# Last head group reordered, its last two heads scaled at Wo's output, and gate and input put into the late tiles' sums early: an attention and MLP gate kernel on one core

## The chip, the cores and the metric

The kernel runs on one core of a Trainium2 chip. The metric is the device time of one execution in microseconds (us), the median of three runs. The core has a matrix engine (PE, which loads weights in a second row called PEld), a vector engine (DVE), an activation engine (ACT), a general engine (POOL), and a queue engine (SP), which issues most transfers.

## The reference

One normalized input feeds an attention over a key and value cache with 32 heads, and a gate made by a two-layer block with shifted channels. The output is the input plus the product of both.

```python
xn = _layernorm(x, axis=-1)                       # x: 1 x 2048 x 512
s = _A_ref(xn, A_k_cache, A_v_cache, A_wq, A_wo)
g = _silu(_B_ref(xn, B_w1, B_w2, B_w3, B_w4))
return x + s * g

def _A_ref(x, k_cache, v_cache, wq, wo):
    q = (lambda x, *d: x.transpose(*d))((x @ wq).reshape(B, Sq, H, Dh), 0, 2, 1, 3)
    scores = jnp.einsum("bhqd,bhkd->bhqk", q, k_cache) * (Dh ** -0.5)
    p = _softmax(scores, axis=-1)
    o = jnp.einsum("bhqk,bhkd->bhqd", p, v_cache)
    return (lambda x, *d: x.transpose(*d))(o, 0, 2, 1, 3).reshape(B, Sq, H * Dh) @ wo
```

There are 2048 queries, 2048 keys, 32 heads of 128 channels, and 512 model channels. The softmax is computed without subtracting a maximum.

## The kernel before, in words

The first stage (before the attention loop) makes the layer norms, the gate for each of 16 tiles of 128 tokens, which stays in `xall`, and the first queries.

The attention is a list of 128 *units*. A unit is one head (`hh`, four in a group) for one block of 512 queries (`qt`, four blocks). The groups `g` run from 0 to 7, and within a group the order is block by block, head by head (`units`, L116). Each unit has eight *slots* (`SPU`), and the main loop (L533) walks slot by slot. The loop's body is the order of instructions on every engine: `pin` keeps instructions in program order, so what stands first in the body goes first on its engine.

In a slot of unit `u`:

- `s_slot` (L272): two score matmuls (called S) of 512 columns into a PSUM tile, and one exponential on ACT into a quarter of the probabilities (`pT`). Two such PSUM tiles rotate.
- `pv_slot` (L302): two value matmuls (called PV), five slots (`LAG`) behind, into `o` of the unit.
- slots 0 and 1: two each of the four matmuls for the next unit's query, and in slot 2 its copy out of PSUM on the DVE (`q_copy`, L264).
- `add_first`, `add_next`, `add_last` (L286 to L300): the DVE sums the probability tiles of the unit down to 128 x 512 in `acc`. The last of them runs in slot 0 of the next unit.
- slot 3: `sums` (L312) of the previous unit. Four matmuls with one column of ones give the sums over keys, the DVE takes reciprocals, and a transfer writes these to memory (`dr`).
- slot 4: `bcast` (L323) reads them back, spread over all 128 partitions (`rb`).
- slot 2: `norm` (L328) of the unit before the previous one. It multiplies `o` with `rb` into `oT`.
- slots 4, 5 and 6: one token tile of Wo's product for a finished block of four heads, by `wo_mm` (L343, four matmuls) and `wo_post` (L358), which adds it into `sacc`. The tiles wait in `wo_todo`.

In the last group `wo_post` also finishes its tile on the DVE: it multiplies by half of the gate (L369), adds the input (L371), which `fin_load` brought by POOL's transfer queue, and SP stores the tile (L372). After the last score slot the loop runs on for three units' length with what is left, and the remaining Wo tiles follow one by one.

PSUM has eight banks: four for the scores, two for `o` (`psO`), one named `xa` that the queries and the sums share, and one named `xm` for Wo.

Of the kernel before, what the change touches and what calls it, by code (L numbers as in the profile page):

```python
# [8 lines left out]
ACT = mybir.ActivationFunctionType  # L9
ALU = mybir.AluOpType  # L10
FP32 = mybir.dt.float32
BF16 = mybir.dt.bfloat16
# [5 lines left out]
def kernel(  # L18
# [26 lines left out]
    QT = Sq // 512  # L45
# [5 lines left out]
    HG = 4  # L51
    NG = H // HG

    SPU = KC // 2
    LAG = 5
# [6 lines left out]
    pin = tc.keep_in_program_order  # L62

    def pool(name, bufs=1, space=None, **kw):
        if space is not None:
            kw["space"] = space
        return tc.tile_pool(name=name, bufs=bufs, **kw)

    ent = ctx.enter_context
    const = ent(pool("const"))  # L70
    xnT = const.tile([P, DC, Sq], BF16, name="xnT")
    xall = const.tile([P, NT, D], BF16, name="xall")
    ones_t = const.tile([P, 1], BF16, name="ones_t")
    nhalf = const.tile([P, 1], FP32, name="nhalf")
    mv1 = const.tile([P, NT, nc.vector.BN_AGGR_DIM], FP32, name="mv1")
    mv2 = const.tile([P, NT, nc.vector.BN_AGGR_DIM], FP32, name="mv2")
# [22 lines left out]
    xsrc = x2d.rearrange("(t p) d -> t p d", p=P)  # L99
# [5 lines left out]
    def mm(out, lhsT, rhs, start, stop):  # L105
        pin(nc.tensor.matmul(out=out, lhsT=lhsT, rhs=rhs, start=start, stop=stop))  # L106

    pin(nc.vector.memset(warm[:], 0.0))
    pin(nc.vector.memset(ones_t[:], 1.0))
    pin(nc.vector.memset(nhalf[:], -0.5))  # L110
    pin(nc.gpsimd.iota(diag[:], pattern=[[-1, P]], base=0, channel_multiplier=1,
                       allow_small_or_imprecise_dtypes=True))
    pin(nc.vector.tensor_scalar(
        out=ident[:], in0=diag[:], scalar1=0.0, scalar2=None, op0=ALU.is_equal))

    units = [(g, qt, hh) for g in range(NG) for qt in range(QT) for hh in range(HG)]  # L116
    NU = len(units)
    NS = NU * SPU
    kTs, vBs, wqs, wos, oTs, st = {}, {}, {}, {}, {}, {}
    todo = defaultdict(list)  # L120

    def at(n, fn):
        todo[n].append(fn)
# [161 lines left out]

    def add_first(u):  # L286
        s = st[u]
        s["acc"] = pB.tile([P, 4, 512], BF16, tag="acc", bufs=2, name="acc")
        pin(nc.vector.tensor_tensor(  # L289
            out=s["acc"][:], in0=s["pT"][0][:], in1=s["pT"][1][:], op=ALU.add))  # L290

    def add_next(u, i):
        a = st[u]["acc"]
        pin(nc.vector.tensor_tensor(out=a[:], in0=a[:], in1=st[u]["pT"][i][:], op=ALU.add))  # L294
# [7 lines left out]
    def pv_slot(u, p):  # L302
        g, qt, hh = units[u]
        s = st[u]
        if p == 0:
            s["o"] = psO.tile([P, 512], FP32, tag="ps_o", name="ps_o")
        pT = s["pT"][p // 2]
        for j in range(2):
            kc = 2 * p + j
            mm(s["o"][:], vBs[g * HG + hh][:, kc, :], pT[:, 2 * (p % 2) + j, :], kc == 0, kc == KC - 1)  # L310
# [10 lines left out]
        pin(nc.sync.dma_start(out=s["dr"][:], in_=rc[:]))  # L321

    def bcast(u):  # L323
        st[u]["rb"] = pB.tile([P, 512], FP32, tag="rb", bufs=2, name="rb")
        pin(nc.sync.dma_start(
            out=st[u]["rb"][:], in_=st[u]["dr"][:].rearrange("p j -> (p j)").partition_broadcast(P)))

    def norm(u):  # L328
        g, qt, hh = units[u]
        s = st.pop(u)  # L330
        if hh == 0:
            oTs[(g, qt)] = pB.tile([P, HG, 512], BF16, tag="oT", bufs=2, name="oT")
        pin(nc.vector.tensor_tensor(  # L333
            out=oTs[(g, qt)][:, hh, :], in0=s["o"][:], in1=s["rb"][:], op=ALU.mult))

    wo_box = {}
    sacc = {}
# [2 lines left out]
        wos[h] = pB.tile([P, D], BF16, tag="wo", bufs=2 * HG, name="wo_h")  # L340
        pin(nc.sync.dma_start(out=wos[h][:], in_=A_wo[h * Dh:(h + 1) * Dh, :]))

    def wo_mm(g, t, hhs, ps=None):  # L343
        if hhs[0] == 0:
            wo_box[0] = psX.tile([P, D], FP32, tag="xm", name="ps_wo") if ps is None else ps
        oT = oTs[(g, t // 4)]
        ts = t % 4
        for hh in hhs:
            mm(wo_box[0][:], oT[:, hh, ts * P:(ts + 1) * P], wos[g * HG + hh][:], hh == 0, hh == HG - 1)

    fin = {}

    def fin_load(t):
        xl = tokp.tile([P, D], BF16, tag="ta", bufs=10, name="xl")
        pin(nc.gpsimd.dma_start(out=xl[:], in_=xsrc[t]))  # L355
        fin[t] = xl

    def wo_post(g, t):  # L358
        ps = wo_box.pop(0)
        if g == 0:  # L360
            sacc[t] = pS.tile([P, D], FP32, tag="sacc", bufs=NT, name="sacc")
            pin(nc.vector.tensor_copy(out=sacc[t][:], in_=ps[:]))
            return
        sa = sacc[t][:]
        pin(nc.vector.tensor_tensor(out=sa, in0=ps[:], in1=sa, op=ALU.add))  # L365
        if g < NG - 1:
            return
        xl, gl = fin.pop(t), xall[:, t, :]
        pin(nc.vector.scalar_tensor_tensor(  # L369
            out=gl, in0=sa, scalar=0.5, in1=gl, op0=ALU.mult, op1=ALU.mult))  # L370
        pin(nc.vector.tensor_tensor(out=xl[:], in0=gl, in1=xl[:], op=ALU.add))  # L371
        pin(nc.sync.dma_start(out=out2d[t * P:(t + 1) * P, :], in_=xl[:]))  # L372

# [121 lines left out]
    pB = left.enter_context(pool("pB", reuse_waits="tile"))  # L495
# [6 lines left out]
    for g in range(NG - 1):  # L502
        b = (g * QT + QT - 1) * HG
        for hh in range(HG):
            h = (g + 1) * HG + hh
# [24 lines left out]
            at(n + 4, lambda: gate_silu(t, th["a"]))  # L530

    wo_todo = deque()
    for n in range(NS + 3 * SPU):  # L533
        u, p = divmod(n, SPU)
        if u < NU:
            g, qt, hh = units[u]
            s_slot(u, p)
        m = n - LAG
        if 0 <= m < NS:
            pv_slot(*divmod(m, SPU))  # L540
        if p in (0, 1) and 4 * HG - 1 <= u < NU - 1:
            q_mm(u + 1, (2 * p, 2 * p + 1))
        if p == 0 and 1 <= u <= NU:
            add_last(u - 1)
        if p == 2 and 4 * HG - 1 <= u < NU - 1:
            q_copy(u + 1)
        if p == 2 and 2 <= u <= NU + 1:
            norm(u - 2)
            if units[u - 2][2] == HG - 1:
                gg, qq = units[u - 2][:2]  # L550
                wo_todo.extend((gg, 4 * qq + ts) for ts in range(4))
                if gg == NG - 1:
                    fin_load(4 * qq)
        if p == 3 and 1 <= u <= NU:
            sums(u - 1)
        if p == 4 and 1 <= u <= NU:
            bcast(u - 1)
        if p in (4, 5) and wo_todo:
            wo_mm(*wo_todo[0], (0, 1) if p == 4 else (2, 3))
        if p == 6 and wo_todo:  # L560
            gg, t = wo_todo.popleft()
            wo_post(gg, t)
            if gg == NG - 1 and t % 4 < 3:
                fin_load(t + 1)
        if p == 4 and u < NU:
            add_first(u)
        if p == 6 and u < NU:
            add_next(u, 2)
        held_mm(n)
        for fn in todo.pop(n, ()):  # L570
            fn()
        if not held and not todo.get(n + 1) and pS is None and n >= 4 * SPU + 5:
            right.close()
            pS = right.enter_context(pool("pS", side="right", reuse_waits="tile"))
    while wo_todo:
        gg, t = wo_todo.popleft()
        wo_mm(gg, t, (0, 1, 2, 3))
        if t not in fin:
            fin_load(t)
        wo_post(gg, t)  # L580
    left.close()
    right.close()

# [29 lines left out]
```

## Time and profile before

| What | us |
|---|---|
| median of three runs | 1286.09 (1286.05 to 1286.43) |
| the profiled execution, its own time | 1285.54 |
| its span in the profile | 1283.8 |
| exponentials on ACT, mean of one (L283, 1024 of them) | 1.027 |
| adds of the probabilities on DVE, mean of one (L294) | 1.221 |
| last add steps on DVE (L299, L300) | 0.692, 0.426 |
| norm on DVE (L333) | 0.681 |
| query copy on DVE (L267) | 0.684 |
| Wo's add on DVE (L365) | 0.692 |
| transfer of reciprocals, out and back, medians | 1.4, 4.1 |
| output store, median from issue to landing | 1.8 |

The span runs from the first instruction to the last event of one profiled execution. The time of that execution lies 1.74 us over its span. A matmul's own duration in the trace includes the filling of the array, so a matmul of 512 columns shows 0.379 us, though the next can start 0.216 us behind it. Groups of instructions are named by line, engine, and output from input. In the chain of waits, each row is the work that the next row waited for.

### The profile page before, as it was taken

Reading aid. Unit: us, or ns where it says so; the run is one execution under the profiler, and the core shown is the slowest. Engines: PE = TensorE matmul, PEld = TensorE weight load, DVE = VectorE, ACT = ScalarE, POOL = GpSimd, SP = SyncE. Lnnn points to the kernel's source line nnn. Section 1 sums busy time; section 2 is a strip of 40 time slices with the busy share of each in tenths; the row PEclk is TensorE's granted clock in tenths of the full one; section 3 lists DMA queues with packets and bytes.
Section 4 is the critical chain, followed back from the end, with each engine's and each line's share of the span. In section 5 each row is a group of like instructions: output and inputs, shape, how many; then the busy total and the mean of one; then the engine's idle time right before and its main releaser. Section 6 shows DMA issues by size and latency. Waiting matters only on the chain.

```text
span 1283.8 us, 16912 instructions
## 1 busy us (share of the span) xinstructions
PE 1263.9 (98%) x6268; PEld 611.3 (48%) x6268; DVE 942.8 (73%) x1316; ACT 1056.8 (82%) x1105; POOL 43.1 (3%) x107
## 2 busy tenths in 40 slices
PE   8999999999999999999999999999999999999996
PEld 4444444444444444444444444444444444444442
DVE  7621567777777777777777777777777777778886
ACT  5444789998888888888888888888888888888882
POOL 4310000000000000000000000000000000000000
PEclk9999999999999999999999999999999999999996
DMA  9391112453144413452144313451244213442221
GB/s 205 56 176 48 24 43 50 82 100 66 33 83 83 83 33 63 79 99 50 42 83 87 70 43 70 79 100 34 50 91 83 58 50 77 80 83 45 63 43 48
DMA packets 169363, 91.05 MB, mean 71 GB/s; under 512 B 122752, under 2 KB 151936, under 8 KB 169280
## 3 DMA queue, kind: packets, MB, share of 16 engines
q1 hardware_dynamic: 165440, 85.24, 33.1%
q0 software_dynamic: 1440, 3.93, 1.4%
q8 instruction: 49, 0.80, 0.3%
q10 hardware_dynamic: 2400, 0.79, 0.2%
q14 instruction: 34, 0.28, 0.1%
HBM read 67.63 MB, written 2.36 MB: 55 GB/s over the span
## 4 chain that ended last, share of the span: by engine, by line
PE 92%; DVE 5%; ACT 1%; DMA 1%; issue 0%; POOL 0%; DVEq 0%; ACTq 0%
PE ps_s L106 37%; PE ps_o L106 35%; PE ps_wo L106 9%; PE ps_q L106 8%; DVE acc L294 2%; PE ps_m L106 2%; PE ps_sum L106 1%; DVE sacc L365 1%; DVE xall L369 1%; DVE acc L299 1%; DVE qT L267 0%; DVE xl L371 0%; DMA rb<-dr 0%; ACT pT L283 0%; ACT xnT L191 0%
## 5 line engine op out<-in xcount | busy, mean ns | idle before, releaser
L283 ACT ACTIVATE pT<-ps_s 128x1024 bf16<-128x1024 f32 x1024 | 993.2, 1027 | 135.2 <-PE ps_s L106 135.2
L106 PE MATMUL ps_s<-qT,kT 128*128 128x512 bf16 x2048 | 609.7, 379 | 1.3 <-ACT pT L283 1.2
L106 PE MATMUL ps_o<-pT,vb 128*128 128x512 bf16 x2048 | 608.4, 379 | 0.0
L294 DVE TENSOR_TENSOR acc<-acc,pT 128x2048 bf16<-128x2048 bf16 x256 | 312.5, 1221 | 72.3 <-ACT pT L283 71.1
L106 PEld LDWEIGHTS <-kT 128*128 128x128 bf16 x2048 | 222.7, 114 | 201.9 <-issue 6.1
L106 PEld LDWEIGHTS <-vb 128*128 128x128 bf16 x2048 | 200.2, 98 | 225.8
L289 DVE TENSOR_TENSOR acc<-pT 128x2048 bf16<-128x2048 bf16 x128 | 156.8, 1225 | 51.1 <-ACT pT L283 51.1
L106 PE MATMUL ps_wo<-wo_h,oT 128*128 128x512 bf16 x512 | 155.6, 388 | 5.4 <-DVE sacc L365 3.1
L106 PE MATMUL ps_q<-xnT,wq_h 128*128 128x512 bf16 x512 | 148.3, 379 | 0.0
L365 DVE TENSOR_TENSOR sacc<-ps_wo,sacc 128x512 f32<-128x512 f32 x112 | 77.5, 692 | 90.0 <-PE ps_wo L106 90.0
L299 DVE TENSOR_TENSOR acc<-acc 128x1024 bf16<-128x1024 bf16 x128 | 88.6, 692 | 4.4
L333 DVE TENSOR_TENSOR oT<-ps_o,rb 128x512 bf16<-128x512 f32 x128 | 87.2, 681 | 1.9 <-DMA rb<-dr 1.9
L106 PEld LDWEIGHTS <-oT 128*128 128x128 bf16 x512 | 50.6, 99 | 69.7 <-issue 8.1
L106 PEld LDWEIGHTS <-wq_h 128*128 128x128 bf16 x512 | 50.0, 98 | 59.6 <-issue 0.3
L267 DVE CAST qT<-ps_q 128x512 bf16<-128x512 f32 x112 | 76.6, 684 | 0.0
L300 DVE TENSOR_TENSOR acc<-acc 128x512 bf16<-128x512 bf16 x128 | 54.5, 426 | 4.4
L106 PEld LDWEIGHTS <-acc 128*128 128x128 bf16 x512 | 37.4, 116 | 34.4 <-issue 4.0
L106 PE MATMUL ps_s<-xn2T,w_sb 128*128 128x512 bf16 x224 | 48.8, 379 | 0.0
L234 ACT ACTIVATE h2T<-ps_s 128x1024 bf16<-128x1024 f32 x28 | 28.7, 1024 | 24.0 <-PE ps_s L106 24.0
L355 POOL DMA_DIRECT2D xl<-in_A_x_dram x16 | 8.7, 542 | 1137.8 <-DMA out_dram<-xl 1012.8
L106 PEld LDWEIGHTS <-w_sb 128*128 128x128 bf16 x304 | 29.7, 98 | 34.6 <-issue 2.1
L319 DVE RECIPROCAL rc<-ps_sum 128x4 f32<-128x4 f32 x128 | 23.3, 182 | 21.2 <-PE ps_sum L106 7.2
(44 smaller groups left out, 331.6 us busy)
## 6 DMA issues: line engine op xcount, KB each, us to landing
rb<-dr SPq DMA_DIRECT2D x128, 256.0 KB, 4.1
vb<-in_A_v_cache_dram SPq DMA_DIRECT2D x64, 256.0 KB, 4.4
wo_h<-in_A_wo_dram SPq DMA_DIRECT2D x32, 128.0 KB, 4.0
wq_h<-in_A_wq_dram SPq DMA_DIRECT2D x28, 128.0 KB, 4.3
w_sb<-in_B_w_dram SPq DMA_DIRECT2D x9, 256.0 KB, 4.7
kT<-in_A_k_cache_dram SPq DMA_TRANSPOSE x128, 4.3
xl<-in_A_x_dram POOLq DMA_DIRECT2D x16, 128.0 KB, 2.3
dr<-rc SPq DMA_DIRECT2D x128, 2.0 KB, 1.4
```

The source lines that it names most:

```text
L106: pin(nc.tensor.matmul(out=out, lhsT=lhsT, rhs=rhs, start=start, stop=stop))
L234: pin(nc.scalar.activation(out=h2[c, f][:], in_=ps[:], func=ACT.Gelu_apprx_tanh))
L267: pin(nc.vector.tensor_copy(out=qT[:], in_=st[u].pop("psq")[:]))
L283: pin(nc.scalar.activation(out=s["pT"][-1][:, jj:jj + 2, :], in_=sps[:], func=ACT.Exp, scale=SCALE))
L289: pin(nc.vector.tensor_tensor(out=s["acc"][:], in0=s["pT"][0][:], in1=s["pT"][1][:], op=ALU.add))
L294: pin(nc.vector.tensor_tensor(out=a[:], in0=a[:], in1=st[u]["pT"][i][:], op=ALU.add))
L299: pin(nc.vector.tensor_tensor(out=a[:, 0:2, :], in0=a[:, 0:2, :], in1=a[:, 2:4, :], op=ALU.add))
L300: pin(nc.vector.tensor_tensor(out=a[:, 0, :], in0=a[:, 0, :], in1=a[:, 1, :], op=ALU.add))
L319: pin(nc.vector.reciprocal(out=rc[:], in_=ps[:]))
L333: pin(nc.vector.tensor_tensor(out=oTs[(g, qt)][:, hh, :], in0=s["o"][:], in1=s["rb"][:], op=ALU.mult))
L365: pin(nc.vector.tensor_tensor(out=sa, in0=ps[:], in1=sa, op=ALU.add))
L369: pin(nc.vector.scalar_tensor_tensor(out=gl, in0=sa, scalar=0.5, in1=gl, op0=ALU.mult, op1=ALU.mult))
```

## The change

The change touches the last head groups only. It has these parts:

- **Order of the last group.** The blocks 2 and 3 (`LATE`) now come first with heads 0 to 2, then the blocks 0 and 1 with all heads, and at the end two single units: head 3 of block 2 (called UA here) and head 3 of block 3 (UB).
- **Wo by heads.** A late block's Wo tiles in the last group sum three heads. Where more than one tile waits in `wo_todo`, units from the tenth-last on take a second tile in slots 0 to 2.
- **One slot later.** From the second unit of the last group to the end of the loop (14 units), norm, sums and the return transfer stand one slot later.
- **Gate and input early.** For late tiles, `sacc` is scaled by half of the gate (`y_scale`) and gets the input (`y_add`) during group 6, after group 5's sum. From group 6 on a late tile's Wo product is multiplied by half of the gate into `tm` and then added, two DVE instructions for one.
- **UA and UB at Wo's output.** Their `o` is copied without a norm (`late_o`). The sums are laid out with one query per partition, by matmuls with the probabilities as weights and a column of twos, so that their reciprocal holds one half. Each head's Wo product is then scaled by that reciprocal per partition and by the gate in one instruction (`late_mul`), or on ACT and POOL for one tile (`late_act`), and added to `sacc` (`late_out`). No reciprocal goes through memory for them. UB's sums take the third and fourth probability tiles directly instead of adding them first.
- **Other engines.** Some final adds go to POOL, two of the last stores to ACT's queue, and the input loads to SP's queue.
- The buffers named `rb` grow from two to five, and `tm` uses them too.

```diff
-    units = [(g, qt, hh) for g in range(NG) for qt in range(QT) for hh in range(HG)]
+    units = [(g, qt, hh) for g in range(NG - 1) for qt in range(QT) for hh in range(HG)]
+    LATE = (QT - 2, QT - 1)
+    GY = NG - 2
+    units += [(NG - 1, qt, hh) for qt in LATE for hh in range(HG - 1)]
+    units += [(NG - 1, qt, hh) for qt in range(QT - 2) for hh in range(HG)]
+    units += [(NG - 1, qt, HG - 1) for qt in LATE]
...
-        pin(nc.gpsimd.dma_start(out=xl[:], in_=xsrc[t]))
+        pin(nc.sync.dma_start(out=xl[:], in_=xsrc[t]))
...
+    def y_scale(t):
+        pin(nc.vector.scalar_tensor_tensor(
+            out=sacc[t][:], in0=sacc[t][:], scalar=0.5, in1=xall[:, t, :], op0=ALU.mult, op1=ALU.mult))
+    def y_add(t):
+        xl = fin.pop(t)
+        pin(nc.vector.tensor_tensor(out=sacc[t][:], in0=sacc[t][:], in1=xl[:], op=ALU.add))
...
+        if t // 4 in LATE and g >= GY:
+            tm = pB.tile([P, D], FP32, tag="rb", bufs=5, name="tm")
+            pin(nc.vector.scalar_tensor_tensor(
+                out=tm[:], in0=ps[:], scalar=0.5, in1=gl, op0=ALU.mult, op1=ALU.mult))
+            pin(nc.vector.tensor_tensor(out=sa, in0=sa, in1=tm[:], op=ALU.add))
+            return
         pin(nc.vector.tensor_tensor(out=sa, in0=ps[:], in1=sa, op=ALU.add))
+        if t // 4 in LATE and g == GY - 1:
+            k = n + SPU * (t - 4 * LATE[0]) + 1
+            at(max(k - SPU, n + 1), lambda: fin_load(t))
+            at(k, lambda: y_scale(t))
+            at(k + SPU, lambda: y_add(t))
...
+    def late_sums(u, src, first, last):
+        ps = st[u]["sum"]
+        for j in range(4):
+            for i, a in enumerate(src):
+                mm(ps[:, j:j + 1], a[:, j * P:(j + 1) * P], twos_t[:],
+                   first and j == 0 and i == 0, last and j == 3 and i == len(src) - 1)
+    def late_o(u, eng):
+        s = st[u]
+        s["ou"] = pB.tile([P, 512], BF16, tag="ou", bufs=2, name="ou")
+        for c in (slice(0, 256), slice(256, 512)):
+            if eng is nc.scalar:
+                pin(eng.activation(out=s["ou"][:, c], in_=s["o"][:, c], func=ACT.Identity))
+            elif c.start == 0:
+                pin(eng.tensor_copy(out=s["ou"][:], in_=s["o"][:]))
+    def late_mul(u, ts, ps):
+        t = 4 * units[u][1] + ts
+        tm = pB.tile([P, D], FP32, tag="rb", bufs=5, name="tm")
+        pin(nc.vector.scalar_tensor_tensor(
+            out=tm[:], in0=ps, scalar=st[u]["rc"][:, ts:ts + 1], in1=xall[:, t, :],
+            op0=ALU.mult, op1=ALU.mult))
+        return tm
+    def late_act(u, ts, ps):
...
+        pin(nc.scalar.activation(out=tm[:], in_=ps, func=ACT.Identity, scale=st[u]["rc"][:, ts:ts + 1]))
+        pin(nc.gpsimd.tensor_tensor(out=tm[:], in0=tm[:], in1=xall[:, t, :], op=ALU.mult))
+        return tm
+    def late_out(u, ts, tm, eng, queue):
+        t = 4 * units[u][1] + ts
+        y = tokp.tile([P, D], BF16, tag="ta", bufs=10, name="y")
+        pin(eng.tensor_tensor(out=y[:], in0=tm[:], in1=sacc[t][:], op=ALU.add))
+        pin(queue.dma_start(out=out2d[t * P:(t + 1) * P, :], in_=y[:]))
...
-    for n in range(NS + 3 * SPU):
+    for n in range(UB * SPU):
         u, p = divmod(n, SPU)
+        extra = u >= NU - 10 and len(wo_todo) > 1
...
+        if p == 0:
+            twice = extra
+        if twice and p < 3:
+            wo_slot(p, n)
...
+        late = u > NU - 4 * HG
+        if p == 2 + late and 2 <= u:
+            norm_queue(u - 2)
-        if p == 3 and 1 <= u <= NU:
+        if p == 3 + late and 1 <= u:
             sums(u - 1)
-        if p == 4 and 1 <= u <= NU:
+        if p == 4 + late and 1 <= u:
             bcast(u - 1)
...
+    for p in range(SPU + LAG):
+        if p < SPU:
+            s_slot(UB, p)
+        pv_slot(*divmod(UB * SPU + p - LAG, SPU))
+        if p == 0:
+            add_next(UA, 3)
+        if p == 1:
+            late_ps(UA)
+            late_sums(UA, [st[UA]["acc"][:, i, :] for i in range(4)], True, True)
+            late_rc(UA)
+        if p == 2:
+            norm_queue(UB - 2)
+            for t in range(1, 4):
+                fin_load(4 * (QT - 3) + t)
+        if p in (3, 6, 8, 10):
+            wo_tile(nc.gpsimd if p < 10 else nc.vector)
+        if p == 4:
+            late_o(UA, nc.vector)
+            add_first(UB)
+        if p == 5:
+            late_tile(UA, 0, bank(psX, "xa"))
+        if p in (5, 7, 9):
+            late_tile(UA, (p - 3) // 2, bank(psO, "ps_o"))
+        if p == 9:
+            late_ps(UB)
+            late_sums(UB, [st[UB]["acc"][:, i, :] for i in range(4)], True, False)
+        if p == 10:
+            late_sums(UB, [st[UB]["pT"][2][:, i, :] for i in range(4)], False, False)
+        if p == 11:
+            late_sums(UB, [st[UB]["pT"][3][:, i, :] for i in range(2)], False, False)
+        if p == 12:
+            late_o(UB, nc.scalar)
+            late_sums(UB, [st[UB]["pT"][3][:, i, :] for i in range(2, 4)], False, True)
+    late_rc(UB)
+    w = [psS.tile([P, 2, 512], FP32, name="ps_s") for _ in range(2)]
+    ws = [w[i // 2][:, i % 2, :] for i in range(4)]
+    for ts in range(4):
+        late_wo(UB, ts, ws[ts])
+    tm = late_act(UB, 0, ws[0])
+    late_out(UB, 0, tm, nc.gpsimd, nc.scalar)
+    tms = {ts: late_mul(UB, ts, ws[ts]) for ts in (1, 2)}
+    late_out(UB, 1, tms[1], nc.vector, nc.sync)
+    tms[3] = late_mul(UB, 3, ws[3])
+    late_out(UB, 2, tms[2], nc.vector, nc.scalar)
+    late_out(UB, 3, tms[3], nc.vector, nc.sync)
```

More of the change, by code (lines that the diff above doesn't have):

```diff
@@ L73 @@
     ones_t = const.tile([P, 1], BF16, name="ones_t")
+    twos_t = const.tile([P, 1], BF16, name="twos_t")
     nhalf = const.tile([P, 1], FP32, name="nhalf")
@@ L109 @@
     pin(nc.vector.memset(ones_t[:], 1.0))
+    pin(nc.vector.memset(twos_t[:], 2.0))
     pin(nc.vector.memset(nhalf[:], -0.5))
@@ L323, in bcast @@
     def bcast(u):
-        st[u]["rb"] = pB.tile([P, 512], FP32, tag="rb", bufs=2, name="rb")
+        st[u]["rb"] = pB.tile([P, 512], FP32, tag="rb", bufs=5, name="rb")
         pin(nc.sync.dma_start(
@@ L341, in load_wo, with wo_mm @@
         pin(nc.sync.dma_start(out=wos[h][:], in_=A_wo[h * Dh:(h + 1) * Dh, :]))
-    def wo_mm(g, t, hhs, ps=None):
+    def wo_mm(g, t, hhs, hn):
         if hhs[0] == 0:
-            wo_box[0] = psX.tile([P, D], FP32, tag="xm", name="ps_wo") if ps is None else ps
+            wo_box[0] = psX.tile([P, D], FP32, tag="xm", name="ps_wo")
         oT = oTs[(g, t // 4)]
@@ L348, in wo_mm @@
         for hh in hhs:
-            mm(wo_box[0][:], oT[:, hh, ts * P:(ts + 1) * P], wos[g * HG + hh][:], hh == 0, hh == HG - 1)
+            mm(wo_box[0][:], oT[:, hh, ts * P:(ts + 1) * P], wos[g * HG + hh][:], hh == 0, hh == hn - 1)
     fin = {}
@@ L354, in fin_load, with wo_post @@
         xl = tokp.tile([P, D], BF16, tag="ta", bufs=10, name="xl")
-        pin(nc.gpsimd.dma_start(out=xl[:], in_=xsrc[t]))
+        pin(nc.sync.dma_start(out=xl[:], in_=xsrc[t]))
         fin[t] = xl
-    def wo_post(g, t):
+    def y_scale(t):
[4 more added lines that the diff above has]
+        pin(nc.vector.tensor_tensor(out=sacc[t][:], in0=sacc[t][:], in1=xl[:], op=ALU.add))
+    def wo_post(g, t, n, eng=nc.vector):
         ps = wo_box.pop(0)
@@ L363, in wo_post @@
             return
-        sa = sacc[t][:]
-        pin(nc.vector.tensor_tensor(out=sa, in0=ps[:], in1=sa, op=ALU.add))
+        sa, gl = sacc[t][:], xall[:, t, :]
+        if t // 4 in LATE and g >= GY:
[4 more added lines that the diff above has]
+            return
@@ L366, in wo_post @@
+        pin(nc.vector.tensor_tensor(out=sa, in0=ps[:], in1=sa, op=ALU.add))
+        if t // 4 in LATE and g == GY - 1:
[3 more added lines that the diff above has]
+            at(k + SPU, lambda: y_add(t))
         if g < NG - 1:
             return
-        xl, gl = fin.pop(t), xall[:, t, :]
+        xl = fin.pop(t)
         pin(nc.vector.scalar_tensor_tensor(
             out=gl, in0=sa, scalar=0.5, in1=gl, op0=ALU.mult, op1=ALU.mult))
-        pin(nc.vector.tensor_tensor(out=xl[:], in0=gl, in1=xl[:], op=ALU.add))
+        pin(eng.tensor_tensor(out=xl[:], in0=gl, in1=xl[:], op=ALU.add))
@@ L372, in wo_post, with late_ps, late_rc @@
         pin(nc.sync.dma_start(out=out2d[t * P:(t + 1) * P, :], in_=xl[:]))
+    def late_ps(u):
+        st[u]["sum"] = psX.tile([P, 4], FP32, tag="xa", name="ps_sum")[:]
+    def late_sums(u, src, first, last):
[4 more added lines that the diff above has]
+                   first and j == 0 and i == 0, last and j == 3 and i == len(src) - 1)
+    def late_rc(u):
+        rc = smp.tile([P, 4], FP32, tag="rl", bufs=2, name="rl")
+        pin(nc.vector.reciprocal(out=rc[:], in_=st[u]["sum"]))
+        st[u]["rc"] = rc
@@ new lines, in late_o, with late_wo @@
+    def late_o(u, eng):
[6 more added lines that the diff above has]
+                pin(eng.tensor_copy(out=s["ou"][:], in_=s["o"][:]))
+    def late_wo(u, ts, ps):
+        h = units[u][0] * HG + units[u][2]
+        mm(ps, st[u]["ou"][:, ts * P:(ts + 1) * P], wos[h][:], True, True)
@@ new lines, in late_mul @@
+    def late_mul(u, ts, ps):
[7 more added lines that the diff above has]
+        t = 4 * units[u][1] + ts
+        tm = pB.tile([P, D], FP32, tag="rb", bufs=5, name="tm")
+        pin(nc.scalar.activation(out=tm[:], in_=ps, func=ACT.Identity, scale=st[u]["rc"][:, ts:ts + 1]))
+        pin(nc.gpsimd.tensor_tensor(out=tm[:], in0=tm[:], in1=xall[:, t, :], op=ALU.mult))
+        return tm
@@ L376 @@
+    def late_out(u, ts, tm, eng, queue):
+        t = 4 * units[u][1] + ts
+        y = tokp.tile([P, D], BF16, tag="ta", bufs=10, name="y")
+        pin(eng.tensor_tensor(out=y[:], in0=tm[:], in1=sacc[t][:], op=ALU.add))
+        pin(queue.dma_start(out=out2d[t * P:(t + 1) * P, :], in_=y[:]))
     for t, eng in enumerate([nc.sync, nc.scalar, nc.sync, nc.scalar]):
@@ L532, with norm_queue, wo_slot @@
     wo_todo = deque()
-    for n in range(NS + 3 * SPU):
+    def norm_queue(u):
+        norm(u)
+        gg, qq, hh = units[u]
+        late = gg == NG - 1 and qq in LATE
+        if hh == HG - 1 - late:
+            wo_todo.extend((gg, 4 * qq + ts, HG - late) for ts in range(4))
+            if gg == NG - 1 and qq not in LATE:
+                fin_load(4 * qq)
+    UA, UB = NU - 2, NU - 1
+    def wo_slot(part, n, eng=nc.vector):
+        gg, t, hn = wo_todo[0]
+        if part < 2:
+            wo_mm(gg, t, (0, 1) if part == 0 else tuple(range(2, hn)), hn)
+            return
+        wo_todo.popleft()
+        wo_post(gg, t, n, eng)
+        if gg == NG - 1 and t % 4 < 3 and t + 1 not in fin and t // 4 not in LATE:
+            fin_load(t + 1)
+    for n in range(UB * SPU):
         u, p = divmod(n, SPU)
-        if u < NU:
-            g, qt, hh = units[u]
-            s_slot(u, p)
+        extra = u >= NU - 10 and len(wo_todo) > 1
+        s_slot(u, p)
         m = n - LAG
@@ L540 @@
             pv_slot(*divmod(m, SPU))
-        if p in (0, 1) and 4 * HG - 1 <= u < NU - 1:
+        if p in (0, 1) and 4 * HG - 1 <= u:
             q_mm(u + 1, (2 * p, 2 * p + 1))
-        if p == 0 and 1 <= u <= NU:
+        if p == 0 and 1 <= u:
             add_last(u - 1)
-        if p == 2 and 4 * HG - 1 <= u < NU - 1:
-            q_copy(u + 1)
[L547 to L553, printed above, removed]
-        if p == 3 and 1 <= u <= NU:
+        if p == 0:
+            twice = extra
+        if twice and p < 3:
+            wo_slot(p, n)
+        if p == 2 and 4 * HG - 1 <= u:
+            q_copy(u + 1)
+        late = u > NU - 4 * HG
+        if p == 2 + late and 2 <= u:
+            norm_queue(u - 2)
+        if p == 3 + late and 1 <= u:
             sums(u - 1)
-        if p == 4 and 1 <= u <= NU:
+        if p == 4 + late and 1 <= u:
             bcast(u - 1)
[L558 to L565, printed above, removed]
+        if p in (4, 5, 6) and wo_todo:
+            wo_slot(p - 4, n)
+        if p == 4:
             add_first(u)
-        if p == 6 and u < NU:
+        if p == 6:
             add_next(u, 2)
@@ L574, with wo_tile, late_tile, bank @@
             pS = right.enter_context(pool("pS", side="right", reuse_waits="tile"))
[L575 to L580, printed above, removed]
+    def wo_tile(eng):
+        for part in range(3):
+            wo_slot(part, NS, eng)
+    def late_tile(u, ts, ps):
+        late_wo(u, ts, ps)
+        late_out(u, ts, late_mul(u, ts, ps), nc.gpsimd, nc.sync)
+    def bank(pl, tag):
+        return pl.tile([P, D], FP32, tag=tag, name="ps_w")[:]
+    for p in range(SPU + LAG):
[14 more added lines that the diff above has]
+            wo_tile(nc.gpsimd if p < 10 else nc.vector)
+        if p == 4:
+            late_o(UA, nc.vector)
[26 more added lines that the diff above has]
+    late_out(UB, 3, tms[3], nc.vector, nc.sync)
     left.close()
```

## Prediction

> **What bounds the kernel now.** I read the page first (share of each engine, then the 40 slices), then the chain of waits in order of time over the last 30 us, then PE's waits and timeline in the last head group.
>
> ```profile
> PE 1263.9 (98%) x6268; PEld 611.3 (48%) x6268; DVE 942.8 (73%) x1316; ACT 1056.8 (82%) x1105; POOL 43.1 (3%) x107
> PEclk9999999999999999999999999999999999999996
> ```
>
> PE is busy for 98% at full clock until the last slice, which holds 0.6 of both. A change can gain by taking work from PE, by closing PE's gaps, or in the last slice. That slice, from the chain of waits (start, length, what):
>
> ```profile
> 1259.88 1.15 DVE acc L294
> ...
> 1264.24 1.42 DMA dr<-rc
> 1265.66 0.02 issue
> 1265.68 3.85 DMA rb<-dr
> 1269.53 0.02 issue
> 1269.56 0.70 DVE oT L333
> ...
> 1276.99 1.88 PE ps_wo L106 x4
> 1278.87 0.02 issue
> 1278.89 0.70 DVE sacc L365
> 1279.62 0.70 DVE xall L369
> 1280.33 0.02 issue
> 1280.35 0.42 DVE xl L371
> ```
>
> PE's dense run ends at 1261.4 (its timeline has the last ten PV matmuls from 1259.10 for 2.32 us). The remaining 22.4 us are a series: the sums of the last unit, a round trip to memory that spreads their reciprocal (1.42 + 3.85), norm, then four tiles of Wo by turns with the DVE, at half clock (four matmuls take 1.88 us). From the last DVE end (1280.77) to the span's end are 3.03 us. Only 20 Wo matmuls, two PV and four sums are real PE work there.
>
> A second, smaller loss is in PE's timeline of the last group; one unit without it, one with it:
>
> ```profile
> 1006.72 0.27 PE L106 MATMUL ps_sum<-ones_t,acc 128*128 128x1 bf16 x4
> 1006.85 0.60 PE L106 MATMUL ps_s<-qT,kT 128*128 128x512 bf16 x2
> 1237.44 0.27 PE L106 MATMUL ps_sum<-ones_t,acc 128*128 128x1 bf16 x4 [0.18 <-DVE qT L267]
> 1237.57 0.60 PE L106 MATMUL ps_s<-qT,kT 128*128 128x512 bf16 x2
> 1246.67 0.60 PE L106 MATMUL ps_s<-qT,kT 128*128 128x512 bf16 x2
> ```
>
> Pairs of 512-column matmuls start 0.431 us apart (0.2155 each) and the four sums cost only 0.13 (1006.72 to 1006.85), so a unit of 40 matmuls and four sums needs 8.75 us. With the wait it takes 9.10 (1237.57 to 1246.67): 0.35 lost. PE's waits list this one 9 times, so 3.15 us. Its cause is the DVE, which in the last group does 1.81 us of final work per tile (0.69 + 0.69 + 0.42) and reaches the query copy late; the sums use the PSUM bank that this copy must empty.
>
> **The change, part by part.** I count in units (one head for 512 queries, eight slots). The last unit, UB, started at 1250.99 before (S in the timeline).
>
> *PE work.* Ahead of UB it is the same: 122 Wo tiles of four matmuls then, now all 128 less four whole tiles and eight single matmuls, 488 both times. In and after UB it was 16 S, 26 PV, 24 Wo and 8 sums; now the same 66 matmuls and 64 sums (16 for UA, 48 for UB: four slices in four columns, and UB's third and fourth probability tiles directly). 56 more sums at 0.13/4 cost +1.8 us. The price is measured on groups of four; if sixteen in a row run slower, the row's 0.27 per four gives 3.8 (+2.0 on my sum).
>
> *The units ahead of UB.* Late tiles lose their final 1.81 us: scale and input add (one each per two units in group 6) and a tile's product and add (two of about 0.69) replace it. The longest DVE unit with one tile is 6.33 (everything but Wo's add: 1.22 + 2 x 1.22 + 0.69 + 0.43 + 0.68 + 0.68 + 0.18) + 1.81 = 8.1 against 8.75 of PE. Units 118, 120, 121 and 124 take two tiles, 122 and 126 none: with two, PE has 44 matmuls, 9.6 us, and the DVE 9.1 (late tiles) or 9.95 (unit 124, tiles 1 and 2). The sums also move one slot later, 0.87 us, more than the 0.35 they were late. So I take back the 3.15. What is late next: in unit 124 the DVE enters 1.5 us late (post and add of the unit ahead), finishes the last add at 3.9, the extra tile at 5.75 and the query copy at 6.4; PE reaches the sums at 6.05: 0.55 with the restart. Units 122 and 126 have no Wo and 0.87 us slots against ACT's 0.93 (six exponentials in 5.61): 0.1 each. Together -3.15 + 0.75 = -2.4: UB starts at 1248.6.
>
> *Queues.* The 16 input loads leave POOL's queue for SP's (0.33 us of issue each). Those of the late tiles wait for buffers freed by the gate's tanh long before, so nothing stands behind them. Behind each output store on SP stand the next reciprocal's two transfers; in unit 124 these land at about 12.4 and norm wants them at 14.3. In UB the slack is only some 0.1 us: sums at 5.3 of a 7.9 us unit, reciprocal 0.2, then 1.42 + 3.85, lands 3.0 us into UB; norm is due at 3.1.
>
> *UB itself*, us from its start. Exponential 7 of UA ends at 1.0, add until 2.2, sums (0.53) wait for it (PE gap 0.55), norm 3.1 to 3.8; Wo of tile 4 ends 5.4; its add and gate product end 6.95; copy of UA's o until 7.65 (PE gap 0.6 at 7.1); add_first 8.9; the products of UA's tiles 0 and 1 until 10.3; tile 5 until 11.7; product 2 until 12.4. PE meanwhile has Wo of tile 5 at 9.9, tile 6 at 12.3, tile 7 at 14.75, sums between, and the last PV at 16.4. So of 16.3 us dense work (66 x 0.2155 + 64 x 0.0325) PE loses some 1.2.
>
> *Behind PE.* ACT copies o in halves: 512 columns take 0.60 and 1024 1.03, so 256 about 0.38: 16.55 to 17.25. Two Wo matmuls land at 17.55, ACT scales tile 0 until 18.2; the DVE's product of tile 1 waits for that ACT instruction (they share a PSUM tile). Then six DVE instructions of 0.70, 18.25 to 22.45, and 3.03 to the end: 25.5. The round trip to memory is gone from the path. A sum of two float32 tiles in SBUF has no row; 0.42 (bf16 add) below, 0.69 (L365) taken, its nearest.
>
> *POOL* adds seven tiles in UB, then multiplies and adds UB's tile 0. The profile has no such POOL operation. Its IOTA of 128 columns takes 0.236 and a MEMSET of 5 0.094: 1.15 ns a column, 0.67 us for 512 in one stream, 1.8 for three (two read, one written). I take 1.3: the queue ends at 17.4, tile 0 at 20.9, ahead of the DVE's 22.45. What these do to DVE instructions that read the same memory is not in the profile either: nothing, or at most a whole POOL instruction each time. I take 1.5 for the two overlaps on the path (add_first with tile 4's add, the first final add with tile 0's multiply).
>
> By the Trainium skill (GPSIMD Engine Reference, section 3.1) a two-input add costs about 2.6 cycles per element at 1.2 GHz, so about 1.1 us plus dispatch as an estimate; the sum would stay as it is. No row here shows it.
>
> *Sum.* 1248.6 + 25.5 + 1.5 = a span of 1275.6, against 1283.8. The profiled execution took 1285.54, 1.74 over its span, and the median of the runs is 0.55 above that: 1275.6 + 1.74 + 0.55 = 1277.9, said as **1278**, 8 us faster (0.6%).
>
> **Rivals.** *DVE late in the last group* (0.12). For it: the nine waits above, and 9.95 us of DVE work in unit 124. Against: the sums' extra slot, and lighter late tiles. If the wait stays in nine units (2.4 more) and four doubled units lose 1 us each: 1284.4, within 0.2%.
>
> *POOL slow* (0.12). With 2.0 us an instruction, its queue from 9.6 on ends at 21.6, tile 0 at 25.6; with 3.03 that is 28.6 for my 25.5 (with the 1.5, 1281.1). For it: nothing here prices POOL. Still faster.
>
> *DVE held by POOL* (0.08), the slow side. Place: UB from 7.0 and the last adds. Eight DVE instructions read two SBUF tiles while POOL is at work (add_first, three gate products, one input add, three final adds). If each waits out a POOL instruction of 1.8, PE, which waits for these in turn for its PSUM banks, stands too: 14.4 less the 1.5 counted, 1290.9. It turns slower than before from a mean wait of 1.2 us each. Against: PE has slack of 1 us at several banks and POOL pauses.
>
> The Trainium skill (GPSIMD Engine Reference, section 1, the specifications) says that POOL shares its SBUF interfaces with VectorE, and names instructions with two SBUF inputs as those that collide; by that rule this rival is the mechanism and its chance would be higher. No run so far has both engines in such work.
>
> That the change doesn't do what it says has no chance of its own: in the changed program's instruction streams late heads 0 to 2 stand first, and the last two units have no transfer to memory.
>
> **How the numbers follow.** Forecast 0.68, own range 1275 (no collision, adds at 0.42, no wait in unit 124) to 1281.5 (sums dear, UB's norm late by 1 us). The three rivals have 0.12, 0.12, 0.08. The range 1275 to 1284.5 leaves out the slow case and some of the forecast's edges. About 0.2% (2.6 us) can be told from no change: faster 0.80 (forecast, slow POOL), same 0.12, slower 0.08.
>
> **What would show it.** UB's first S near 1248.6; no query-copy wait before the sums but in unit 124; no memory round trip in the chain after 1260; PE dense to about 1265; last DVE end about 1272.5; POOL rows of 128x512 near 1.3. It is wrong if PE's gaps in the last unit pass 5 us, if the chain ends through POOL, or if the sums in rows of 16 cost over 0.07 each.

## The result and the profile after

The changed kernel takes 1278.88 us (median of four runs, 1277.92 to 1279.8) against 1286.07 beside it: a ratio of 0.9944 (95% interval 0.9926 to 0.9961), 7.2 us faster. The executions of both kernels lie in two groups some 1.6 us apart (two of these four in the later one), and the difference is there before the attention begins, at the first activation of the gate's block (54.8 to 55.4 us in one group, 56.5 to 56.6 in the other, from a cause that stays open), so what the first stage ran later is taken off where traces are compared. The profiled execution took 1278.11 with a span of 1276.3, 7.5 below the span before.

The page of the changed kernel, share of each engine and granted clock in 40 slices:

```profile
PE 1253.6 (98%) x6199; PEld 611.3 (48%) x6324; DVE 957.4 (75%) x1333; ACT 1056.4 (83%) x1108; POOL 46.5 (4%) x100
...
PEclk9999999999999999999999999999999999999998
```

The last slice holds 0.8 of the clock where it had 0.6. DVE's busy time went up by 14.6 us while its instructions grew by 17 only; 4.2 of the 14.6 are seen below as stretched instructions.

PE's waits from 1100 us to the end (us in total, times, longest):

```profile
PE ps_w L107 <- DVE ou L424: 0.4, 1, 0.4
...
PE ps_sum L107 <- DVE qT L274: 0.2, 1, 0.2
```

The longest wait is now 0.4, for UA's copied `o`. The wait of the sums for the query copy is there once, at 1228.52 in unit 124, where it was there nine times. The chain of waits at the end (start, length, what):

```profile
1264.54 0.47 PE ps_o L107 x2
...
1265.03 0.39 ACT ou L422
...
1265.47 1.05 PE ps_s L107 x4
1266.52 1.38 issue
1267.90 0.70 ACT tm L441
```

No transfer to memory is left in it. PE is dense until its last value matmuls at 1264.5 to 1265.0. Then UB's four Wo matmuls run, and at 1266.52 they are done. But ACT, which has to scale the first tile with the reciprocal, begins at 1267.90: 1.38 us of "issue", in which the chain shows nothing. The timeline of the last unit shows what it is (start, length, engine, line, instruction; rows of PE, DVE and POOL). First the row of the kernel before with which UB starts, then the changed kernel's:

```profile
1250.99 0.59 PE L106 MATMUL ps_s<-qT,kT 128*128 128x512 bf16 x2
```

```profile
1248.92 0.59 PE L107 MATMUL ps_s<-qT,kT 128*128 128x512 bf16 x2
...
1255.87 1.15 POOL L397 TENSOR_TENSOR xl<-xall,xl 128x512 bf16<-128x512 bf16 x1 [1182.89 <-ACT pT L290]
1256.25 1.85 DVE L296 TENSOR_TENSOR acc<-pT 128x2048 bf16<-128x2048 bf16 x1
...
1261.84 1.15 POOL L397 TENSOR_TENSOR xl<-xall,xl 128x512 bf16<-128x512 bf16 x1
1262.04 1.49 DVE L395 SCALAR_TENSOR_TENSOR xall<-sacc,xall 128x512 bf16<-128x512 f32 x1
...
1264.62 1.14 POOL L397 TENSOR_TENSOR xl<-xall,xl 128x512 bf16<-128x512 bf16 x1
1264.83 1.50 DVE L395 SCALAR_TENSOR_TENSOR xall<-sacc,xall 128x512 bf16<-128x512 f32 x1
1265.73 1.71 POOL L448 TENSOR_TENSOR y<-tm,sacc 128x512 bf16<-128x512 f32 x1
1266.35 1.37 DVE L397 TENSOR_TENSOR xl<-xall,xl 128x512 bf16<-128x512 bf16 x1
1267.65 0.17 DVE L414 RECIPROCAL rl<-ps_sum 128x4 f32<-128x4 f32 x1
...
1269.89 1.26 POOL L448 TENSOR_TENSOR y<-tm,sacc 128x512 bf16<-128x512 f32 x1
1270.02 1.69 DVE L448 TENSOR_TENSOR y<-tm,sacc 128x512 bf16<-128x512 f32 x1
```

UB starts at 1248.92, 2.07 earlier than before (2.4, since this execution's first stage ran 0.3 later), and from there to the end it takes 27.4 us instead of 32.8. The DVE reaches UB's reciprocal only at 1267.65, because the instructions ahead of it are stretched: the add of probabilities takes 1.85 where the mean is 1.227, two gate products 1.49 and 1.50 where others of the unit take 0.69, an input add 1.37 for 0.42, and after it a final add 1.69 for 0.64.

Each stretched instruction began while POOL was in an add, and ended its own time after POOL's end, less 0.1:

| DVE instruction | begins | POOL's ends | plus its own time | it ended |
|---|---|---|---|---|
| add of probabilities L296 | 1256.25 | 1257.02 | 1258.24 | 1258.10 |
| gate product L395 | 1262.04 | 1262.99 | 1263.68 | 1263.53 |
| gate product L395 | 1264.83 | 1265.76 | 1266.45 | 1266.33 |
| input add L397 | 1266.35 | 1267.44 | 1267.86 | 1267.72 |
| final add L448 | 1270.02 | 1271.15 | 1271.79 | 1271.71 |

It goes the other way too: POOL's add at 1265.73 began inside the product that ended at 1266.33 and took 1.71, where one alone takes 1.26 (1266.33 + 1.26 = 1267.59, it ended at 1267.44). DVE instructions with one input in PSUM (L386, L433) keep their 0.67 to 0.74 beside POOL.

By the Trainium skill (SBUF — State Buffer, "Who interferes with whom") the two engines share one pair of SBUF ports under an exclusive lock: a DVE instruction with two SBUF inputs contends with a POOL instruction that reads SBUF, and one with at most one SBUF input, outside the two-port modes, does not. That whoever is first holds the pair for its whole instruction, while the other blocks, the Trainium skill says there of the two-port modes; the table shows it for two SBUF inputs, to 0.15 us.

### The profile page after: what moved, and what is told of

Read it like the earlier page. It is cut to its first block, busy times and chain, and to the rows that moved or that the text cites. A ratio compares the mean times of both kernels' runs of the same rounds, so it can differ in the third digit from the quotient of the medians.

```text
span 1276.3 us, 16933 instructions
## 1 busy us (share of the span) xinstructions
PE 1253.6 (98%) x6199; PEld 611.3 (48%) x6324; DVE 957.4 (75%) x1333; ACT 1056.4 (83%) x1108; POOL 46.5 (4%) x100
## 3 DMA queue, kind: packets, MB, share of 16 engines
q10 hardware_dynamic: 2688, 1.05, 0.3%
## 4 chain that ended last, share of the span: by engine, by line
PE 95%; ACT 2%; DVE 2%; issue 1%; DMA 0%; DVEq 0%; ACTq 0%
PE ps_s L107 38%; PE ps_o L107 37%; PE ps_wo L107 8%; PE ps_q L107 8%; PE ps_m L107 2%; PE ps_sum L107 1%; ACT pT L290 1%; DVE acc L301 0%; PE ps_warm L107 0%; DMA kT<-in_A_k_cache_dram 0%; ACT xnT L198 0%; DVE xall L395 0%; DVE sacc L386 0%; ACT qT L276 0%; DVE acc L306 0%
## 5 line engine op out<-in xcount | busy, mean ns | idle before, releaser
L107 PE MATMUL ps_s<-qT,kT 128*128 128x512 bf16 x1989 | 597.4, 380 | 3.7 <-ACT pT L290 1.2
L296 DVE TENSOR_TENSOR acc<-pT 128x2048 bf16<-128x2048 bf16 x128 | 157.0, 1227 | 49.0 <-ACT pT L290 49.0
L107 PE MATMUL ps_wo<-wo_h,oT 128*128 128x512 bf16 x500 | 149.2, 379 | 0.1
L107 PE MATMUL ps_q<-xnT,wq_h 128*128 128x512 bf16 x485 | 142.8, 379 | 0.1
L386 DVE TENSOR_TENSOR sacc<-ps_wo,sacc 128x512 f32<-128x512 f32 x96 | 66.4, 691 | 69.4 <-PE ps_wo L107 69.4
L397 POOL TENSOR_TENSOR xl<-xall,xl 128x512 bf16<-128x512 bf16 x3 | 3.4, 1148 | 1182.9 <-ACT pT L290 1182.9
L326 DVE RECIPROCAL rc<-ps_sum 128x4 f32<-128x4 f32 x126 | 23.0, 183 | 27.4 <-PE ps_sum L107 14.3
```

The lines of the kernel that those rows point to most:

```text
L296: pin(nc.vector.tensor_tensor(out=s["acc"][:], in0=s["pT"][0][:], in1=s["pT"][1][:], op=ALU.add))
L326: pin(nc.vector.reciprocal(out=rc[:], in_=ps[:]))
L397: pin(eng.tensor_tensor(out=xl[:], in0=gl, in1=xl[:], op=ALU.add))
```

## The experiments

Times are medians. The changed kernel's own over five runs is 1278.05, 8.20 below the kernel before beside it (1286.25).

**The changed kernel again**, as the base for the others.

> The changed kernel once more, as the measure for the others of this batch. Main theory: about 1278.9, single runs between 1277.9 and 1279.8 as before; the DVE instructions of the last unit that read two SBUF tiles take 0.5 to 1.0 us longer than elsewhere where POOL adds at the same time (input add of tile 7 1.37 for 0.42, gate products 1.5 for 0.69). Rival (the longer DVE instructions are chance): they are not longer in this trace.

It took 1278.05 (1277.90 to 1278.09; ratio 0.9937, 0.9925 to 0.9949). The long instructions are in its trace too (1.85, 1.49, 1.50, 1.37, 1.69), so they are no chance of one execution.

**POOL's adds on the DVE.** Seven final adds and input adds of the last unit go to the DVE; UB's tile 0 stays on POOL.

```diff
-        late_out(u, ts, late_mul(u, ts, ps), nc.gpsimd, nc.sync)
+        late_out(u, ts, late_mul(u, ts, ps), nc.vector, nc.sync)
...
-            wo_tile(nc.gpsimd if p < 10 else nc.vector)
+            wo_tile(nc.vector)
```

> The seven adds that POOL does in the last unit are done by the DVE; POOL keeps only the multiply and add of the last unit's tile 0. Collision theory: add_first of the last unit takes 1.22 instead of 1.85, the gate products 0.69 instead of 1.5, tile 7's input add 0.42 instead of 1.37, in all 3.2 us less, against seven more DVE adds (3 x 0.42 + 4 x 0.65 = 3.9): the reciprocal starts 0.7 us later, the time changes by less than 1.2 us. Rival (these DVE instructions are slow for another reason, POOL has no part): they stay long and the time rises by 3.9 us.

1279.28 (1278.82 to 1280.63; 0.9949, 0.9935 to 0.9962), 1.2 us slower than the changed kernel. Its timeline, DVE:

```profile
1256.78 1.22 DVE L296 TENSOR_TENSOR acc<-pT 128x2048 bf16<-128x2048 bf16 x1
...
1267.74 0.69 DVE L395 SCALAR_TENSOR_TENSOR xall<-sacc,xall 128x512 bf16<-128x512 f32 x1
1268.47 0.43 DVE L397 TENSOR_TENSOR xl<-xall,xl 128x512 bf16<-128x512 bf16 x1
...
1271.12 1.76 DVE L448 TENSOR_TENSOR y<-tm,sacc 128x512 bf16<-128x512 f32 x1
```

Without POOL beside them, all instructions ahead of the reciprocal have their own length again; the final add, which still meets POOL's add of tile 0, has 1.76. That is the collision, shown by its cause: with POOL's adds gone the stretch is gone. But seven adds on the DVE itself (three of 0.42, four of 0.69, 4.0 in all) cost more than the 3.2 of stretching that they end, and the reciprocal comes 1.1 later (at 1268.81, with a first stage 0.1 later) for the 0.7 expected. POOL was worth using all the same.

**The reciprocal first.** UB's reciprocal is put ahead of tile 7's gate product and input add, of which the product follows right behind it, where the DVE would wait for ACT, and the add behind the next two products.

```diff
+        if t == 7:
+            rest.extend((gate, store))
+            return
...
     late_rc(UB)
+    rest[0]()
...
     tms = {ts: late_mul(UB, ts, ws[ts]) for ts in (1, 2)}
+    rest[1]()
```

> The last unit's reciprocal stands ahead of tile 7's gate product and input add on the DVE; these run between the last products. Theory (the reciprocal waits 2.2 us behind DVE work that the collisions stretch, and the sums are ready at 1265.1 from the span's start): the reciprocal starts at about 1265.4 for 1267.65, ACT's scaling at 1266.1, the DVE ends about 1.4 us earlier, time 1.0 to 1.8 us less. Rival (the end is set by DVE's total work alone, in any order): less than 0.4 us.

1276.99 (1276.89 to 1278.42; 0.9931, 0.9919 to 0.9944), 1.06 less than the changed kernel. Its timeline, DVE (this execution's first stage ran 1.5 later):

```profile
1266.73 0.18 DVE L425 RECIPROCAL rl<-ps_sum 128x4 f32<-128x4 f32 x1 [0.42 <-PE ps_sum L107]
1266.83 1.01 DVE L398 SCALAR_TENSOR_TENSOR xall<-sacc,xall 128x512 bf16<-128x512 f32 x1
```

The reciprocal now waits for PE's sums and stands at 1266.73 - 1.5 = 1265.2, 2.4 earlier than in the changed kernel: so much did the stretched queue hold it. Only 1.06 of the 2.4 reaches the end: ACT's scaling now waits for PE's Wo product and starts at 1267.63 - 1.5 = 1266.1, 1.8 earlier, and the two instructions now run behind the reciprocal, the first of them stretched to 1.01 again.

**Without the later slot.** `late = False`, all else as changed.

```diff
-        late = u > NU - 4 * HG
+        late = False
```

> Norm, sums and return transfer of the last group are put back into slots 2, 3 and 4. Theory (the waits of the sums for the query copy went because the late tiles' DVE work is lighter AND because of the slot; the extra tiles of four units make the DVE late again without it): the wait returns in the units with an extra tile and behind those with final work, 4 to 6 units, 0.35 to 1.3 us each, 2 to 4 us in all. Rival (lighter late tiles alone removed it): at most two units, under 0.8 us. Rival (the slot alone): nine units as before, 3.2 us.

1280.97 (0.996, 0.9947 to 0.9972), 2.9 slower. PE's waits:

```profile
PE ps_sum L107 <- DVE qT L274: 2.6, 6, 1.1
```

The lighter late tiles alone leave the wait in six units, up to 1.1 long; the later slot is what clears it.

**The later slot alone**, in the kernel before.

```diff
+        late = NU - 4 * HG < u < NU - 1
-        if p == 2 and 2 <= u <= NU + 1:
+        if p == 2 + late and 2 <= u <= NU + 1:
```

(and so for the sums and the return transfer)

> The kernel before with one part alone: in the last group norm, sums and return transfer stand one slot later (units 113 to 126). Theory (the nine waits for the query copy cost 0.35 each with PE's restart): all nine go, the first score of the last unit comes at about 1247.9 for 1251.0, 3.1 us less, 1283.1. Rival (only the idle time that the waits' view lists, 0.18 each): 1.6 us less. Rival (the wait comes back at the later place): under 0.5 us less.

1283.48 against 1286.17 (ratio 0.9978, 0.9969 to 0.9987), 2.7 us faster. PE's waits from 1100 us on, all rows:

```profile
PE ps_wo L106 <- DVE oT L333: 3.8, 1, 3.8
PE ps_wo L106 <- DVE sacc L365: 3.1, 4, 0.8
PE ps_sum L106 <- DVE acc L300: 2.5, 2, 2.2
```

The nine waits for the query copy are gone. From first score to first score, units 118 to 126 took 9.10 before, where a unit without the wait took 8.77; now they take 8.80, and so do the other units in the later slot. So each wait cost 0.33, and the later slot 0.03 in each of its 14 units. These three lines are the tail. By itself the slot is worth about a third of what the whole change gains.

**UB through memory again.** Its o, sums, reciprocals and norm go the way of the kernel before, with a scale of one half behind; order and all else as changed.

```diff
-    late_rc(UB)
+            sums(UB)
+            bcast(UB)
...
+    pin(nc.vector.tensor_tensor(out=st[UB]["ou"][:], in0=st[UB]["o"][:], in1=st[UB]["rb"][:], op=ALU.mult))
```

> The last unit alone goes back to the old way: its probabilities are added up on the DVE, its sums' reciprocal goes through memory and is spread, o is multiplied by it, then Wo, with 0.5 as the scale. Theory (the round trip on the path is what the change removed, and nothing hides it): the DVE has 3.6 us more (1.22 + 1.22 + 0.69 + 0.42), the sums come at about 1269, then 1.4 + 3.9 to memory and back, norm 0.7, Wo, and the same six last instructions: 7 to 9 us more than 1278.1, so 1285 to 1287. Rival (the DVE's backlog of tile 7 and the other late tiles covers the trip): under 3 us more.

1289.38 (1288.95 to 1290.91; 1.0025, 1.0016 to 1.0035), 11.3 more than the changed kernel and slower than the kernel before. Its chain of waits:

```profile
1270.21 1.15 DVE acc L301
...
1272.59 0.31 PE ps_sum L107 x4
...
1273.13 1.40 DMA dr<-rc
...
1274.55 4.07 DMA rb<-dr
```

That is more than the 7 to 9 expected. The round trip is 5.5 of it, and norm and Wo, which now stand behind it, are 1.7. The rest is that the adds of UB's probabilities now stand on the DVE behind tile 7's stretched instructions, so that even its sums begin at 1272.6 (1271.1 with 1.5 of a later first stage taken off), where the changed kernel has them done by 1265.2; the reciprocal starts 3.8 later. Scaling at Wo's output is therefore more than a shortcut around the transfers: taking the probabilities as weights also takes the last adds off the DVE.

**The sums twice.** Every `late_sums` matmul is issued twice, with ones for twos, so that the reciprocals still hold one half.

```diff
+        src = src + src
...
-                mm(ps[:, j:j + 1], a[:, j * P:(j + 1) * P], twos_t[:],
+                mm(ps[:, j:j + 1], a[:, j * P:(j + 1) * P], ones_t[:],
```

> All 64 late sums are done twice, with ones for twos, so 64 matmuls of one column more. Theory (0.033 us each, and the last unit's end is set by the DVE, 2.2 us behind the sums): the trace shows 32 sums in about 1.05 us, PE's last PV 1.6 to 2.1 us later, the time at most 0.8 us more than 1278.1. Rival (0.067 us each): 4.3 us more on PE, the reciprocal late, the time 2 us or more above.

1278.35 (0.9938, 0.9925 to 0.9952), 0.3 more. PE's timeline:

```profile
1261.89 0.94 PE L107 MATMUL ps_sum<-ones_t,acc 128*128 128x1 bf16 x32
1262.90 0.38 PE L107 MATMUL ps_o<-pT,vb 128*128 128x512 bf16 x1
```

32 sums with the weight loads between them hold PE for 1.0 us at most, 0.03 each. The last value matmuls move by 1.4 (1264.40 to 1265.62, with a first stage 0.2 earlier) for the 1.6 to 2.1 expected, and the reciprocal by only 0.4 (1267.87): in the changed kernel it is the DVE that sets it, not PE.

**A version with less to collide ahead of the reciprocal.** Block 1's tiles get gate and input early as well, so the last unit has no gate product and no input add left. Its final adds go to POOL, but for UB's tiles 1 to 3; UB's tile 0 is multiplied on the DVE, with the four product tiles in banks of their own, and two more `rb` buffers.

```diff
+    EARLY = (QT - 3, QT - 2, QT - 1)
...
-            wo_tile(nc.gpsimd if p < 10 else nc.vector)
+            wo_tile(nc.gpsimd)
...
-    ws = [w[i // 2][:, i % 2, :] for i in range(4)]
+    ws = [bank(psO, "ps_o"), w[0][:, 0, :], w[1][:, 0, :], w[1][:, 1, :]]
...
-    tm = late_act(UB, 0, ws[0])
+    tms = [late_mul(UB, ts, ws[ts]) for ts in range(4)]
```

> A version built on the findings: gate and input go early into the tiles of block 1 too (their last sums need one product on the DVE and one add on POOL), so the last unit's DVE has no gate product or input add left; its reciprocal no longer waits; the last four products stand in a row and tile 0 takes DVE and POOL without ACT. Theory: reciprocal at about 1265.3 for 1267.6, the DVE ends at about 1271.0 for 1273.5, time about 1275.5. Rival (POOL with eight float32 adds of 1.3 to 1.7 becomes the bound): POOL ends behind the DVE, 1277 or more.

1276.17 (0.9924, 0.9911 to 0.9936). From UB's start to the last DVE end it took 21.0 us instead of 24.65, but UB started 1.85 later: in eight units of groups 5 and 6 the additional scaling and adding made the query copy late for the sums, and they took 8.92 to 9.06 instead of 8.77. One stretched add is left, 1.70 for 1.22 beside POOL's first add, 3.6 us ahead of the sums that read it. So the later slot was begun with group 5:

```diff
-        late = u > NU - 4 * HG
+        late = u > NU - 10 * HG
```

> x1 with the later slot for norm, sums and return transfer from unit 89 on instead of 113. In x1 eight units of groups 5 and 6, which got the early scale and add of block 1, ran 8.9 to 9.2 us for 8.77 and put the last unit 1.85 us later. Theory (the same wait of the sums for the query copy): all units of groups 5 and 6 take 8.77 to 8.80, the last unit's first score comes 1.85 us earlier, time 1274.3. Rival (the DVE has too much work in these units, whatever the slot): less than 0.5 us from 1276.2.

**1275.04** (1274.95 to 1275.49; 0.9914, 0.9901 to 0.9928), 10.9 below the kernel before beside it and the best of all. Its timeline, DVE and POOL:

```profile
1259.30 9.84 POOL L454 TENSOR_TENSOR y<-tm,sacc 128x512 bf16<-128x512 f32 x8 [1.88 <-DVE tm L437]
...
1265.67 0.18 DVE L418 RECIPROCAL rl<-ps_sum 128x4 f32<-128x4 f32 x1 [0.88 <-PE ps_sum L107]
...
1269.06 1.89 DVE L454 TENSOR_TENSOR y<-tm,sacc 128x512 bf16<-128x512 f32 x3
```

The DVE waits for PE's sums before the reciprocal, no longer the other way about; eight POOL adds in a row have 1.23 each, the last three DVE adds 0.63 each, and UB's tail is again 21.0 us. What it fell short of is ahead of UB: units in the later slot take 8.80 instead of 8.77, 0.7 over the 24 more of them. They take it in the kernel before with the slot alone, too, so it goes with the slot; why stays open.

## Why the prediction came out right

The median is 0.9 us over the predicted one, inside its range and on its side; the five later runs of the same kernel have 1278.05. By its steps:

- **Units ahead of UB, -2.4.** Measured -2.4 with the first stage's 0.3 taken off (UB at 1248.92 for 1248.6), but not by these parts alone. The 15 units of the last group ahead of UB took 132.46 us for 134.57, 2.1 less; the other 0.3 came in the groups ahead of it, and why stays open. The slot alone gave 2.6 there in the kernel before (131.97) for the 3.15 that I took back, because a unit in the later slot takes 0.03 more. The other parts cost 0.5 for 0.75: unit 124 took 10.03, 0.37 over the work of its 44 matmuls, where I gave it 0.55, and units 122 and 126 took 8.02, 0.08 over theirs. Units 118, 120 and 121 have 42 matmuls and not 44, since a late tile sums three heads, and took 9.23 without a wait.
- **Sums, +1.8 us of PE work.** Right in size, 0.03 each also in rows of 16 and 32. It was off the path, though: doubling them cost 0.3 us.
- **UB on PE.** The last value matmul ended at 16.1 us from UB's start for 16.4. The return transfer did not keep its slack of 0.1: it took 4.5 us for 3.85, and norm waited 0.69 for it and began at 3.6 for 3.1. PE did not wait for that, since only the last of the four matmuls of Wo's first tile needs this norm, and the tile was done at 5.4 as predicted.
- **Behind PE.** The order was right, also the DVE's wait for ACT's scaling in the shared PSUM tile (0.87). The DVE's end was predicted at 1272.55 and came at 1273.57; from there to the span's end are 2.73 for 3.03.
- **POOL.** 1.15 (bf16) and 1.26 (float32) for the 1.3 taken, and up to 1.72 where its add met a DVE instruction. "POOL slow" did not happen.
- **Collisions, 1.5: the term that was mis-sized.** I counted two places. On the DVE ahead of the reciprocal there were four, 0.63 + 0.80 + 0.81 + 0.94 = 3.2, three of them on work of tiles 6 and 7 that stood only in the rival, and one of 1.05 after it. Of the 3.2, 2.4 reached the reciprocal and 1.8 reached ACT's scaling, which without them waits for PE (the run with the reciprocal first). So 2.8 stand against 1.5. The sum still held within 0.4 us of span, because the smaller things went the other way: PE was done 0.4 earlier, the last six DVE instructions took 0.4 less than predicted apart from the 1.05, and the end after the last of them was 0.3 shorter. That the total came so close is in part luck.

Of the rivals, *DVE late in the last group* is refuted as it stands; without the later slot the wait comes back in six units, and the change would have lost 2.9 us of its gain. *DVE held by POOL* named the right mechanism: an instruction waits out POOL's. Over the eight instructions that it named, the mean was 0.53 us (4.2 in all), under the 1.2 from which it would have turned the sign. Three of the eight met no running POOL instruction or began first.

The largest part of the gain is the tail, 5.4 of 7.5 us. In the run through memory the same order is 3.2 us slower than the kernel before, so as it is built here it needs the scaling at Wo's output. What the new order, or gate and input early, would be worth by itself was not run.

## What to carry to other kernels

In these runs an add moved to POOL was free only where the DVE's instructions beside it have an input in PSUM; where both their inputs are in SBUF, count up to the whole POOL instruction for each that begins after it, and above all for those ahead of something short that the end waits for, such as a reciprocal. Put that short instruction first, or move the work to where nothing waits for it: the last version, with gate and input of block 1 in groups 5 and 6, has 3.65 less in the tail. Part of that may be its other changes, tile 0 off ACT and tile 7's last add on POOL; and the units that took the work needed the later slot, which cost 0.7 us. And where PE waits a little in many units for a copy that is late by less than a slot, move the waiting instruction one slot back before making the copy's engine lighter.

## What was not expected of the hardware

Matmuls with one column, each with a weight load of its own, follow each other at 0.03 us also in rows of 16 or 32, though the weight loads from `acc` are listed with a mean of 0.114 each. Doubling all 64 of them cost 0.3 us here. They also replace adds on the DVE: in the run through memory, where the last unit's adds stand there again, its sums come some 6 us later.
